# Sparse attention and a squared-ReLU expert on one core: half of the early casts moved into DMA transfers, and the masks of both halves made by VectorE products

## The chip, the cores and the metric

The kernel runs on one core of a Trainium2 chip. The metric is the device time of one execution in microseconds (us). Lower is better. Executions of one kernel lie within about 1.5% of each other. An execution more than 1.5% above the fastest of its kernel counts as slow and is not used. "Same" means a difference of less than 2%.

Words used below. PE is the matrix engine, DVE is VectorE, ACT is ScalarE, POOL is GpSimd, and SP is SyncE, which here only issues transfers. A *granted clock* of 1.00 means that PE ran at its full rate, and 0.5 that it got half of it. A *filler* is a matmul on zeros whose result nobody reads (`keep_warm`). It is there to keep PE busy. The *transposed q* of a batch (`qb<-scr_q`) comes, from batch 2 on, by a transposing transfer from a buffer in DRAM (`scr_q`), and the scores of that batch wait for it.

## The reference, cut to what matters

```python
# q, k, v: 8 batches x 8 heads x 576 tokens x 64, fp32; 8 global tokens; window 32
scores = q @ k.T / 8
mask = |i - j| <= 32  or  i is global  or  j is global
attn = softmax(where(mask, scores, -1e9))
x = (attn @ v) as 4608 tokens x 512          # heads side by side
h = x @ w_in                                 # 512 -> 2048
out = (relu(h) ** 2) @ w_out                 # 2048 -> 512, fp32
```

The expert's matmuls fill most of the time, and they can start only when the attention of the first half of batch 0 is done. The values of the global tokens are needed by every query, and the outputs of the global queries are written over their columns of x at the end (`scatter`).

## The kernel before: the parts that matter

Batch 0 (8 heads, handled as 4 pairs) is the start-up. Its k and q come as fp32 through transfers issued by SP, and DVE and ACT cast them. Then come transposes on PE, scores, exponentials, and outputs.

```python
for hp in range(NHP):                    # all 4 pairs of batch 0, fp32
    for nm in "kq":
        fetch_tokens(nc.sync, nm, 0, hp)
...                                      # cut: constants by affine_select on GpSimd
for x in range(NT):
    fetch_values(0, x)                   # GpSimd issues; the transfer casts to fp16
```

The mask of half 0 was added in PSUM by an identity matmul ahead of the scores. That of half 1 was multiplied in by DVE after the exponential.

```python
def mask_first(half, tag):
    sc = pst(tag, [P, 2, 512])
    for e in range(2):
        nc.tensor.matmul(sc[:, e, 0:W], identity, far[:, 0:W], start=True, stop=False, ...)
```

The values of the global tokens of batch 0 were gathered by one-hot matmuls, and copied by ACT and DVE (`v_globals`, one call for each pair). The global columns of x are written by `scatter`, whose columns are register values. They are loaded from SBUF by VectorE in `load_columns`, after two clamps each in `columns`.

```python
def load_columns(part):
    idx, top = {None: (g32c, S - 1), 0: (g32a, HS), 1: (g32b, S - 256)}[part]
    _, gvs[part] = nc.values_load_multi_w_load_instructions(
        idx[0:1, 0:NG], engines=[mybir.EngineType.DVE], ...)

def scatter(b, part=None, pairs=slice(0, NHP)):
    for g in range(NG):
        dve.tensor_copy(out=xT[:, pairs, lo:hi][:, :, ds(gvs[part][g], 1)],
                        in_=gxs[b][:, pairs, g : g + 1])
```

The order of the start-up, cut:

```python
mask_natural(0); gb = indices(); fetch_globals(); keep_warm(4); one_hots(gb); ...
cast_tokens(dve.tensor_copy, "k", 0); cast_tokens(act.copy, "q", 0)
mask_globals(mg, 0); transposes0(0); mask_added(0)
for nm in "kq":
    cast_tokens(dve.tensor_copy, nm, 1)          # pair 1
for i in range(4): pool.dma_start(out=w_in...)
for i in range(NHP):                             # transposes, scores, exp; keep_warm(1) each
    ...
for j in range(4): pool.dma_start(out=w_out...)
mask_natural(1); columns(); clear_ones(dve.memset, vb[0]); load_columns(0)
...                                              # outputs of half 0, with keep_warm(1) each
scatter(0, 0)
...                                              # batch 1's k, q, v are fetched from here on
scatter(0, 1)
take(99)                                         # expert matmuls of the queue
globals_in_place()                               # casts batch 1's and 2's global rows (DVE, ACT)
value_globals(1)                                 # SP: 5 small transfers into vb of batch 1
globals_to_scratch(2); tokens_to_scratch(2)
```

The softmax here doesn't subtract the row's maximum and nothing guards it: scores larger than these inputs give would overflow.

Of the kernel before, what the change touches and what calls it, by code (L numbers as in the profile page):

```python
# [42 lines left out]
SCHED = dict(h0=0, w=4, h1=2, h2=2, h3=0, p0=3, p1=1, p2=2, b1=((2, 1, 2), (1, 1, 2), (1, 1, 2), (1, 1, 2)))  # L43
# [4 lines left out]
def kernel(  # L48
# [41 lines left out]
    st = {nm: sbt("st" + nm, [TP, H, TJ, D], FP32) for nm in "kq"}  # L90
# [21 lines left out]
    def fetch_values(b, x, hs=slice(0, H)):  # L112
        back = NG if b == 0 and x else 0
        pool.dma_start(  # L114
            out=vb[b][NG - back : NG + KN[x], x, 2 * hs.start : 2 * hs.stop : 2],
            in_=v[b, hs, x * KT - back : x * KT + KN[x]].rearrange("h s d -> s h d"),
        )

    act.dma_start(out=g64, in_=global_idx.unsqueeze(0))
    for hp in range(NHP):  # L120
        for nm in "kq":
            fetch_tokens(nc.sync, nm, 0, hp)
    act.preload_act_table_set("natural_log_exp_and_others")

# [6 lines left out]
    pidx = sbt("pidx", [P, 4], I32)  # L131
    nc.gpsimd.iota(pidx, pattern=[[0, 4]], base=0, channel_multiplier=1)
    icb = sbt("icb", [P, 4], I32)
    nc.gpsimd.iota(icb, pattern=[[2 * H * S, 4]], base=2 * H * S, channel_multiplier=0)
    ig = sbt("ig", [P, NG], FP32)
    nc.gpsimd.iota(
        ig, pattern=[[1, NG]], base=0, channel_multiplier=0, allow_small_or_imprecise_dtypes=True,
    )

    U0 = 48  # L140
    UN = 208
    ub = [sbt(f"ub{i}", [P, UN], FP16) for i in range(2)]
    nc.gpsimd.memset(ub[0], 1.0)
    for base, cu, cm in (
        (-8, 0, 1), (window + U0 - 8, -1, 1), (window - U0 + 8, 1, -1),
    ):
        nc.gpsimd.affine_select(
            out=ub[0], in_=ub[0], compare_op=ALU.is_ge, fill=0.0,
            base=base, pattern=[[cu, UN]], channel_multiplier=cm,
        )  # L150
    rows = sbt("rows", [P, 2], FP16)
    nc.gpsimd.memset(rows, 1.0)
    for col, base, cm in ((slice(0, 2), -8, 1), (slice(1, 2), KN[-1] + 7, -1)):
        nc.gpsimd.affine_select(
            out=rows[:, col], in_=rows[:, col], compare_op=ALU.is_ge, fill=0.0,
            base=base, pattern=[[0, col.stop - col.start]], channel_multiplier=cm,
        )
    nc.gpsimd.affine_select(
        out=ub[1], in_=ub[0], compare_op=ALU.is_ge, fill=0.0,
        base=KN[-1] + 7, pattern=[[0, UN]], channel_multiplier=-1,  # L160
    )

    tok = sbt("tok", [P, NT], FP32)
    nc.gpsimd.iota(
        tok, pattern=[[KT, NT]], base=-8, channel_multiplier=1,
        allow_small_or_imprecise_dtypes=True,
    )
    nc.gpsimd.affine_select(
        out=tok, in_=tok, compare_op=ALU.is_ge, fill=-1.0,
        base=-8, pattern=[[0, NT]], channel_multiplier=1,  # L170
    )
    tokp = sbt("tokp", [P, TJ], FP32)
    nc.gpsimd.iota(
        tokp, pattern=[[1, TJ]], base=0, channel_multiplier=TJ,
        allow_small_or_imprecise_dtypes=True,
    )
    identity = sbt("identity", [P, P], FP16)
    nc.gpsimd.memset(identity, 0.0)
    nc.gpsimd.affine_select(
        out=identity, in_=identity, compare_op=ALU.not_equal, fill=1.0,  # L180
        base=0, pattern=[[-1, P]], channel_multiplier=1,
    )
    for kt in kts:
        dve.memset(kt[:, 4, 8 + KN[4] : P], 0.0)
# [4 lines left out]

    def clear_tail(op, t):  # L190
        op(t[96:P, NT - 1, 0 : 2 * H : 2], 0.0)

    clear_tail(dve.memset, vb[0])
    for x in range(NT):
        fetch_values(0, x)
# [78 lines left out]
    far = sbt("far", [P, SCW[0]], FP16)  # L274

# [12 lines left out]

    def mask_added(half):

        r = slice(MB[half], MB[half] + SCW[half])
        nc.vector.tensor_scalar(
            out=far[:, r], in0=mask[:, r], scalar1=-1.0, scalar2=100.0 / scale,
            op0=ALU.add, op1=ALU.mult,
        )



# [65 lines left out]
    grows = sbt("grows", [NG, 3, 2, H, D], FP32, bufs=2, tag="gt")  # L364
    grow = {nm: grows[:, i] for i, nm in enumerate("kqv")}
    g16s = {nm: sbt("g16s" + nm, [NG, 2, H, D], FP16) for nm in "kqv"}

    def fetch_globals():
# [3 lines left out]
        )  # L372
        for nm in "kqv":
            for g in range(NG):
                nc.sync.dma_start(
                    out=grow[nm][g : g + 1],
                    in_=src[nm][1:3, :, ds(at[g], 1), :].rearrange("b h o d -> o b h d"),
                )
# [74 lines left out]
    def v_globals(hp, op1=None, op2=None):  # L453
        vs = vb[0][:, :, 4 * hp : 4 * hp + 4 : 2]
        gl = pst("mm", [P, 512])[0:NG, 0 : 2 * D]
        for t in range(NT):
            nc.tensor.matmul(gl, oh[:, t, :], vs[:, t], start=(t == 0), stop=(t == NT - 1))
        gvs = sbt("gvs", [NG, 2 * D], FP16, bufs=2)
        (op1 or act.copy)(out=gvs, in_=gl)
        (op2 or dve.tensor_copy)(  # L460
            out=vs[0:NG],
            in_=gvs.rearrange("p (h d) -> p h d", d=D).unsqueeze(1).to_broadcast((NG, NT, 2, D)),
        )

    def transposed(nm, i, tag):
        b, hp = divmod(i, NHP)
        tr = pst(tag, [P, 1024], FP16)
        for j in range(TJ):
            n = TP + NG if (b and j == TJ - 1) else TP
            if b == 0:  # L470
                nc.tensor.transpose(
                    tr[:, TP * j : TP * j + n], nat0[(nm, hp)][:, j, :], identity[0:n, 0:n]
                )
            for e in range(2) if b else ():
# [5 lines left out]
        if b == 0:  # L480
            gl = tr.bitcast(FP32)[:, 384 : 384 + NG]
            for j in range(TJ):
                nc.tensor.matmul(
                    gl, nat0[(nm, hp)][:, j, :], ohp[0:TP, j, :],
                    start=(j == 0), stop=(j == TJ - 1), skip_group_check=True,
                )
# [134 lines left out]
    def mask_first(half, tag):  # L621
        sc = pst(tag, [P, 2, 512])
        W = SCW[half]
        for e in range(2):
            nc.tensor.matmul(
                sc[:, e, 0:W], identity, far[:, 0:W],
                start=True, stop=False, skip_group_check=True,
            )
        return sc

    def scores(i, half, tag, wins, sc=None):
        kt, qt = key_query(i)
        added = sc is not None
        if not added:
            sc = pst(tag, [P, 2, 512])
        for t, so, c0, w in wins[half]:
            for e in range(2):
# [3 lines left out]
                    start=not added, stop=True, skip_group_check=True,  # L641
# [3 lines left out]
    def weights(half, sc, wins, added=False):  # L645
# [5 lines left out]
        if not added:  # L651
            dve.tensor_tensor(  # L652
                out=et[:, :, 0:W], in0=et[:, :, 0:W],
                in1=mask[:, MB[half] : MB[half] + W].unsqueeze(1).to_broadcast((P, 2, W)),
                op=ALU.mult,
            )
# [275 lines left out]
```

## Time and profile before

| | before |
|---|---|
| time, median of 3 | 331.81 us (331.32 to 332.03) |
| span in the profile | 330.1 us |
| PE busy / DVE busy / ACT busy | 316.8 / 223.9 / 212.9 us |
| first expert matmul on tokens | 27.31 us |
| first scores of batch 2 | 69.66 us |
| mean granted clock | 0.999 |

The table of stretches of the kernel before has, for each stretch of time: its length, the busy time of each engine with the number of its instructions, the granted clock of PE, the mean busy share of the DMA engines, and GB/s.

```profile
0.00:8.25 8.25, 5.75 (x41) 2.37 (x42) 6.00 (x36) 4.06 (x11) 7.03 (x24) 1.00 0.79 210
8.25:16.50 8.25, 7.33 (x130) 5.11 (x130) 6.81 (x24) 6.24 (x18) 7.12 (x9) 1.00 1.79 196
16.50:24.75 8.25, 6.18 (x114) 4.40 (x114) 5.87 (x23) 5.67 (x19) 2.42 (x4) 1.00 1.27 205
...
41.00:50.00 9.00, 8.23 (x111) 5.54 (x112) 6.09 (x16) 5.87 (x13) 6.73 (x8) 1.00 2.23 161
...
70.00:330.00 260.00, 255.58 (x1616) 126.63 (x1610) 172.16 (x440) 166.98 (x320) 72.86 (x84) 1.00 0.90 99
```

The first number after the length is PE. In the last 260 us PE is 98% busy, so there is little to gain there. In the first 70 us it has gaps. The timeline of PE shows where it waits. A line gives start, length, engine, source line, operation, its tiles, and in brackets the idle time just before it and what ended that.

```profile
6.18 0.43 PE L471 MATMUL mm<-identity,nat0k 96*128 96x96 f16 x6
...
7.74 0.55 PE L625 MATMUL sc<-far,identity 128*128 128x456 f16 x2 [0.59 <-DVE far L292]
...
17.85 0.26 PE L672 MATMUL sc<-et,vb 128*64 128x160 f16 x2 [0.69 <-DVE vb L460]
...
27.31 1.92 PE L543 MATMUL mm<-xT,w_in 128*128 128x256 f16 x16
...
39.47 0.45 PE L475 MATMUL tr<-identity,natk 96*64 96x96 f16 x12 [0.51 <-DMA natk<-in_k_dram]
...
46.69 0.23 PE L672 MATMUL sc<-et,vb 128*64 128x88 f16 x2 [0.17 <-DMA vb<-in_v_dram]
...
49.10 0.25 PE L672 MATMUL acc<-et,vb 128*64 128x136 f16 x2 [0.52 <-DMA vb<-in_v_dram]
```

In the first 18 us of the start-up PE waits mostly for DVE, in pieces of at most 0.7 us. The last three lines are the waits for batch 1's data, 1.2 us in all, that the change aims at. The timeline of VectorE has the casts of pairs 0, 1 (k and q) and, later, the scatter of half 1 and the cast of the value rows of the global tokens:

```profile
5.36 0.77 DVE L449 CAST nat0k<-stk 96x768 f16<-96x768 f32 x1
...
7.61 0.54 DVE L449 CAST nat0k<-stk 96x768 f16<-96x768 f32 x1
8.51 0.56 DVE L449 CAST nat0q<-stq 96x768 f16<-96x768 f32 x1 [0.36 <-DMA stq<-in_q_dram]
...
34.30 1.65 DVE L751 COPY xT<-gx 128x4 f16 x8
...
37.95 0.68 DVE L383 CAST g16sv<-grows 8x1024 f16<-8x1024 f32 x1
```

The timeline of SyncE's queue has the five transfers that put these rows beside batch 1's values:

```profile
38.66 3.87 SPq L440 DMA_DIRECT2D vb<-g16sv  x5
```

### The profile page before, as it was taken

What the parts mean: (1) busy time and instruction counts of PE and PEld (TensorE: products, weight loads), DVE (VectorE), ACT (ScalarE), POOL (GpSimd) and SP (SyncE); (2) the same over time, 40 slices, a digit from 0 to 9 for tenths busy, and PEclk for the clock granted to TensorE, in tenths of its full rate; (3) what the DMA queues carried; (4) which work ended last, traced back from release to release, by engine and by line L of the source; (5) the groups of instructions that cost most, each with busy time, mean ns of one, the idle gap of its engine ahead of it and who ended that gap; (6) DMA issues with size and microseconds to landing.
All of it is one profiled execution on the core that took longest, in us unless ns stands there. A gap on an engine that the chain in (4) does not pass through costs nothing.

```text
span 330.1 us, 6785 instructions
## 1 busy us (share of the span) xinstructions
PE 316.8 (96%) x2393; PEld 165.4 (50%) x2393; DVE 223.9 (68%) x610; ACT 212.9 (64%) x425; POOL 107.6 (33%) x140
## 2 busy tenths in 40 slices
PE   6878999999999999999999999999999999999996
PEld 2656764445454545554545554545555444444444
DVE  7877965787768775877587758775887585323421
ACT  4767666669953995499549954995499536404700
POOL 8822477008900792077006920690000000000000
PEclk9999999999999999999999999999999999999999
DMA  7999999946998299999932999999610001011012
GB/s 210 196 205 208 202 160 140 150 143 68 138 148 192 19 138 161 170 105 128 158 124 52 125 139 159 140 127 158 111 66 1 32 34 64 0 66 64 1 47 82
DMA packets 148876, 38.20 MB, mean 116 GB/s; under 512 B 136818, under 2 KB 144362, under 8 KB 148842
## 3 DMA queue, kind: packets, MB, share of 16 engines
q0 software_dynamic: 104624, 17.37, 70.9%
q1 hardware_dynamic: 44072, 20.26, 31.1%
q8 instruction: 19, 0.31, 0.4%
q10 hardware_dynamic: 146, 0.13, 0.1%
q14 instruction: 15, 0.12, 0.1%
HBM read 37.36 MB, written 17.05 MB: 165 GB/s over the span
## 4 chain that ended last, share of the span: by engine, by line
PE 46%; ACT 23%; DVE 12%; DMA 9%; issue 6%; POOL 2%; SPq 0%; DVEq 0%; ACTq 0%; POOLq 0%
PE mm L587 22%; ACT rl L529 9%; PE mm L524 9%; ACT et L648 7%; PE tr L587 5%; DMA vb<-in_v_dram 5%; ACT rec L704 4%; DMA qb<-scr_q 4%; DVE xT L732 3%; PE tr L524 3%; ACT rec L705 2%; DVE et L652 2%; DVE xT L751 2%; PE sc L681 2%; DVE gt L530 2%
## 5 line engine op out<-in xcount | busy, mean ns | idle before, releaser
L587 PE MATMUL mm<-w_out,gt 128*128 128x512 f16 x448 | 104.9, 379 | 0.0
L524 PE MATMUL mm<-xT,w_in 128*128 128x512 f16 x384 | 90.8, 379 | 0.6 <-DVE xT L751 0.6
L587 PEld LDWEIGHTS <-gt 128*128 128x128 f16 x560 | 52.1, 98 | 58.1
L524 PEld LDWEIGHTS <-w_in 128*128 128x128 f16 x512 | 47.5, 98 | 53.9 <-issue 1.1
L529 ACT ACTIVATE rl<-mm 128x512 f16<-128x512 f32 x96 | 55.1, 600 | 26.4 <-PE mm L524 25.8
L530 DVE TENSOR_TENSOR gt<-rl 128x512 f16<-128x512 f16 x128 | 52.2, 423 | 16.6 <-ACT rl L529 14.4
L648 ACT ACTIVATE et<-sc 128x880 f16<-128x880 f32 (+1 forms) x32 | 29.0, 905 | 43.4 <-PE sc L639 43.4
L652 DVE TENSOR_TENSOR et<-et,mask 128x880 f16<-128x880 f16 x60 | 36.6, 615 | 26.8 <-ACT et L648 25.9
L114 POOL DMA_DIRECT2D vb<-in_v_dram x40 | 41.7, 1620 | 7.9 <-DMA w_out<-in_moe_w_out_dram 6.9
L524 PE MATMUL tr<-xT,w_in 128*128 128x512 f16 x128 | 32.9, 380 | 0.0
L564 DVE COPY ot<-mm 128x512 f32<-128x512 f32 (+1 forms) x29 | 19.7, 679 | 17.5 <-PE mm L587 15.8
L732 DVE TENSOR_TENSOR xT<-sc,rec 64x288 f16<-64x288 f32 (+1 forms) x56 | 25.5, 455 | 8.8 <-ACT rec L705 8.4
L890 POOL COPY pin<-gsh 1x1 f32<-1x1 f32 x5 | 0.9, 178 | 89.1 <-DVE gsh L720 89.1
L705 ACT ACTIVATE rec<-rec 128x288 f32<-128x288 f32 x64 | 28.3, 442 | 2.0
L648 ACT ACTIVATE et<-acc 128x880 f16<-128x880 f32 (+1 forms) x32 | 29.0, 908 | 0.2 <-PE acc L639 0.2
L732 DVE TENSOR_TENSOR xT<-acc,rec 64x288 f16<-64x288 f32 (+1 forms) x56 | 25.5, 455 | 5.1 <-ACT rec L705 4.7
L681 PEld LDWEIGHTS <-vb 128*128 128x128 f16 x288 | 21.4, 98 | 12.6 <-issue 2.0
L419 POOL DMA_DIRECT2D scr_k<-in_k_dram x30 | 26.6, 1098 | 2.6 <-DMA natq<-in_q_dram 1.7
L704 ACT ACTIVATE rec<-sc 64x288 f32<-64x288 f32 (+1 forms) x56 | 22.8, 407 | 6.5 <-PE sc L681 4.2
L587 PE MATMUL tr<-w_out,gt 128*128 128x512 f16 x112 | 25.3, 379 | 0.0
L419 POOL DMA_DIRECT2D scr_q<-in_q_dram x24 | 24.9, 1591 | 0.7 <-DMA vb<-in_v_dram 0.6
L704 ACT ACTIVATE rec<-acc 64x288 f32<-64x288 f32 (+1 forms) x56 | 22.6, 404 | 1.9 <-PE acc L672 1.1
(135 smaller groups left out, 297.2 us busy)
## 6 DMA issues: line engine op xcount, KB each, us to landing
out_dram<-ot SPq DMA_DIRECT2D x35, 256.0 KB
vb<-in_v_dram POOLq DMA_DIRECT2D x29, 120.0 KB, 10.9
scr_q<-in_q_dram POOLq DMA_DIRECT2D x24, 144.0 KB, 5.5
scr_k<-in_k_dram POOLq DMA_DIRECT2D x24, 120.0 KB, 4.2
w_in<-in_moe_w_in_dram POOLq DMA_DIRECT2D x4, 512.0 KB, 14.1
w_out<-in_moe_w_out_dram POOLq DMA_DIRECT2D x4, 512.0 KB, 17.5
stk<-in_k_dram SPq DMA_DIRECT2D x4, 288.0 KB
stq<-in_q_dram SPq DMA_DIRECT2D x4, 288.0 KB
```

The costliest lines, as they stand in the source:

```text
L114: pool.dma_start(out=vb[b][NG - back : NG + KN[x], x, 2 * hs.start : 2 * hs.stop : 2], in_=v[b, hs, x * KT - back : x * KT + KN[x]].rearra ...
L419: pool.dma_start(out=scr[(nm, b % 2)][x * pitch + off : x * pitch + off + hi - lo].rearrange("s (h d) -> s h d", d=D), in_=src[nm][b, :, l ...
L524: nc.tensor.matmul(ph, w_in[:, t, u * P : (u + 1) * P], xT[:, t, XOFF + c * TC : XOFF + (c + 1) * TC], start=(t == 0), stop=(t == NDM - 1),)
L529: nc.scalar.activation(out=rl, in_=ph, func=AF.Relu)
L530: nc.vector.tensor_tensor(out=gts[c][:, u, :], in0=rl, in1=rl, op=ALU.mult)
L587: nc.tensor.matmul(po, gts[c][:, f, m * P : (m + 1) * P], w_out[:, f, :], start=(f == 0), stop=(f == NFF - 1),)
L648: act.activation(out=et[:, :, 0:W], in_=sc[:, :, 0:W], func=AF.Exp, bias=0.0, scale=scale)
L652: dve.tensor_tensor(out=et[:, :, 0:W], in0=et[:, :, 0:W], in1=mask[:, MB[half] : MB[half] + W].unsqueeze(1).to_broadcast((P, 2, W)), op=AL ...
L681: nc.tensor.matmul(acc[:, e, o : o + w], vtf[:, t, vo : vo + P], et[:, e, so : so + w], start=(n == 0), stop=(n == nw - 1), skip_group_che ...
L704: act.activation(out=rec[r], in_=av[rs, xs, :, 0:GTOK], func=AF.Ln)
L705: act.activation(out=rec, in_=rec, func=AF.Exp, scale=-1.0)
L732: dve.tensor_tensor(out=xT[r, hp, x0 : x0 + HS].rearrange("p (k x) -> p k x", k=2), in0=av[r, x, :, 0:GTOK], in1=rec[r], op=ALU.mult,)
```

## The change

The intent is to take work off the engines of the start-up. Half of batch 0's k and q (pairs 2 and 3) comes by transfers that cast, so that four DVE casts go. The mask of half 0 becomes a VectorE product like that of half 1, so that eight identity matmuls go. The value rows of batch 0's global tokens are fetched directly, and cast once on ACT, so that 20 matmuls and four chains of copies go. Batch 1's k, q and v are transferred ahead of w_out. The constants are made by DVE from iotas, and GpSimd starts its transfers earlier. The fillers and the order of units were set anew. The diff, cut to its core:

```diff
-    for hp in range(NHP):
+    for hp in range(2):
         for nm in "kq":
             fetch_tokens(nc.sync, nm, 0, hp)
...
-    (constants by affine_select on GpSimd)
+    (iotas on GpSimd)
+    for nm in "kq":
+        fetch_tokens(pool, nm, 0, 2, 2)
+    for x in range(NT):
+        fetch_values(0, x)
+    def constants():                    # DVE: identity, ub, rows, tok
...
-    def mask_first(half, tag): ...
-        (weights(): no product when the mask was added)
+        dve.tensor_tensor(out=et..., in0=et..., in1=mask..., op=ALU.mult)   # always
...
-    def v_globals(hp, op1=None, op2=None): (one-hot matmuls, ACT and DVE copies)
+    def v_globals():
+        act.copy(out=gv16, in_=gv0)
+        for x in range(NT):
+            dve.tensor_copy(out=vb[0][0:NG, x, 0 : 2 * H : 2], in_=gv16)
...
+    constants()
     one_hots(gb)
     cast_tokens(dve.tensor_copy, "k", 0)
     cast_tokens(act.copy, "q", 0)
+    mask_natural(0)
+    transposes0(0)
+    mg = mask_globals_matmul(0)
+    mask_globals(mg, 0)
+    columns()
+    load_columns(0)
+    cast_tokens(dve.tensor_copy, "k", 1)
+    cast_tokens(dve.tensor_copy, "q", 1)
+    keep_warm(SCHED["w3"])
+    tr_k(1, ...); keep_warm(SCHED["w4"]); tr_q(1, ...)
...
+    (w_in, then batch 1's k, q and v, then w_out)
+    v_globals()
+    half0(2); half0(3)
+    half0_out(0, "mm"); half0_out(1, "sc"); half0_out(2, "acc"); half0_out(3, "mm")
...
-            dve.tensor_reduce(out=gsum[b][:, half, hp], ...)
+            for x in range(2):
+                dve.tensor_reduce(out=gsum[b][:, half, hp, x], ...)
```

## The prediction

> **What bounds it now.** The page gives PE 96% busy of a 330.1 us span at full granted clock, but the shortfall sits at the front. In the timeline of PE the first expert matmul on real tokens starts at 27.3 us; before it PE does batch 0's attention (half of it) and warm-up matmuls. From 70 us on PE is busy 97 to 99% (stretch table), and nothing in the change removes matmuls there, so I take that part as constant. DMA is the second limit: in the records of single transfers the 16 engines are busy from 3.2 us until about 58 us without a gap: batch 0 k and q (1536-byte packets, 178 to 200 per us, to 11.6), v (128-byte, 1120 per us, landed 16.66), w_in and w_out (190 per us, to 37), batch 1 k/q (260 per us, to 43), batch 1 v (to 47, last piece waited for until 49.1), then batch 2. Batch 2's transposed q lands near 68.3; PE uses it at 69.66, so only about 1.3 us of slack.
>
> **What changes.** (1) Half of batch 0's k and q arrives by casting transfers: 768 packets at 260 per us instead of 178 to 200, about 1.2 us less engine time. The Trainium skill ("DMA: Bandwidth & Descriptors", SWDGE vs HWDGE vs iDMA) says each engine round-robins between queues; this trace differs: v, issued from 4.7 us, moved its first packet only at 11.5, when the direct queue was empty. By that order v should land at about 14.7 instead of 16.66. (2) Batch 1 k/q/v go ahead of w_out: at 31 and 35 us instead of 43 and 47. That removes PE's waits for DMA at 39.5, 46.7 and 49.1 (0.51+0.17+0.52 = 1.2 us). (3) Removed: mask matmuls (8, about 0.27 each) and the 20 value-global matmuls with four chains of ACT 0.26 and DVE 0.4; four DVE casts of 0.56. (4) Added: four DVE mask products of 0.64, VectorE constants (about 1.7 us before the one-hots), a doubled tensor_reduce (60 more of 0.19), index arithmetic and clears moved to the batch-1 units.
>
> **Critical path.** I chained the new order with durations of the trace. Constants delay the first k cast by about 0.6 us; pair 1 casts wait behind masks; exps of pairs 2 and 3 wait on ACT behind q copies and the value-global cast. First half-0 output: about 18.8 us (before 17.85), although v is early: ACT and DVE bind, not v. Then four Ln/Exp pairs, scatter (1.65 us) and products as before: expert matmuls start near 27.4, about where they did. So the start gains nothing, the DMA waits give 1.2 us back, and more DVE work in 50 to 70 us (about 3 us, PE already waits for DVE 1.1 us there) takes about 0.5. The doubled reduces fall into DVE's wait for the Exp (0.28 us). Net about -0.7, a little more allowed for tuned fillers: **330.6 us, 327.8 to 333.2**. Faster by over 2%: 5%; within: 91%; slower: 4%.
>
> **What would show it.** v landing 14 to 15.5; first expert matmul 26 to 29; no PE wait for a DMA between 35 and 50; DVE busy about 235 us (223.9 now); the span after 70 us unchanged within 0.7 us.
>
> **What would make it wrong.** Global value rows landing late (32 small SP transfers at 0.75 us each instead of 24), stalling ACT at the value-global cast, or DVE's cast of batch-1 globals near 36 us; a start 2 to 3 us earlier because DVE/ACT overlap better than chained; batch 2's transposed q landing after PE wants it.

One correction to its text. The times of single transfers in it (3.2, 11.6, 37, 43, 47, 58 and 68.3 us) were read with a zero that lay 1.35 us too early, so they are about 1.35 us too high on the scale of the other views. Differences between two of them are not touched. But the slack of 1.3 us for batch 2's transposed q sets 68.3 against 69.66 from the timeline of PE, so on one scale it is about 2.7 us. And the direct queue was not quite empty when the first packet of v moved: 70 of its 1536 packets were still to come.

## The result, and the profile after

| | before | after |
|---|---|---|
| time, median of 4 | 331.56 us (330.60 to 332.03) | 334.77 us (334.06 to 335.48) |
| ratio | | 1.010 (1.0067 to 1.0134) |
| span in the profile | 330.1 us | 333.7 us |
| PE / DVE / ACT busy | 316.8 / 223.9 / 212.9 us | 319.6 / 230.7 / 211.4 us |
| first half-0 outputs | 17.85 us | 19.35 us |
| first expert matmul on tokens | 27.31 us | 28.68 us |
| first scores of batch 2 | 69.66 us | 73.43 us |
| mean granted clock, each run | 0.999 (profiled run) | 0.974 in all four |

A ratio is the mean time of one kernel's fast runs over that of the other's of the same rounds, with its 95% interval, so it is not quite the ratio of the two medians. The changed kernel is 1.0% slower. That is "same" by the 2% rule, but it is outside the predicted range, whose upper end was 333.2 us.

The table of stretches of the kernel after:

```profile
0.00:8.25 8.25, 5.93 (x41) 2.47 (x41) 5.85 (x35) 3.48 (x10) 7.48 (x22) 1.00 0.86 194
8.25:16.50 8.25, 6.49 (x129) 4.91 (x131) 5.36 (x17) 3.73 (x12) 4.83 (x7) 0.66 1.81 179
16.50:24.75 8.25, 7.28 (x134) 6.18 (x133) 6.91 (x27) 6.79 (x14) 4.09 (x5) 0.52 1.27 204
...
41.00:50.00 9.00, 7.24 (x98) 5.42 (x99) 6.87 (x20) 6.21 (x13) 5.03 (x6) 0.91 1.93 174
...
70.00:330.00 260.00, 258.56 (x1632) 128.04 (x1630) 177.40 (x500) 168.09 (x324) 72.72 (x84) 1.00 0.90 97
```

Read the clock column first: 0.66 and 0.52 where it was 1.00. The last line is not a slower steady state. The kernel after reaches 70 us with more work left (1632 instead of 1616 matmuls remain), and does it at the same rate. The timeline of PE after, with the answers to the lines shown above:

```profile
6.67 0.60 PE L195 MATMUL tr<-idle 128*128 128x512 f16 x2
9.25 0.43 PE L453 MATMUL mm<-identity,nat0k 96*128 96x96 f16 x6 [1.97 <-DVE nat0k L435]
...
13.92 0.69 PE L457 MATMUL mm<-identity,natk 96*64 96x96 f16 x12
...
19.35 0.34 PE L648 MATMUL mm<-et,vb 128*64 128x160 f16 x2 [0.67 <-DVE vb L444]
...
39.05 1.92 PE L528 MATMUL mm<-xT,w_in 128*128 128x256 f16 x16 [0.66 <-DVE xT L729]
...
46.63 0.26 PE L648 MATMUL sc<-et,vb 128*64 128x160 f16 x2 [0.44 <-DVE gt L540]
...
48.02 0.27 PE L648 MATMUL sc<-et,vb 128*64 128x192 f16 x2 [1.05 <-DMA vb<-g16sv]
...
48.64 0.28 PE L648 MATMUL sc<-et,vb 128*64 128x88 f16 x2 [0.27 <-DMA vb<-g16sv]
```

Three things are to be seen. There is one wait of 1.97 us at 9.25 us, for the cast of pair 1's k. The transposes at 13.92 us took 0.69 us for twelve, against 0.45 for the same form in the kernel before. The waits for batch 1's tokens and values are gone, as intended, but there are new ones in the same place: for the *global rows* of the values (`vb<-g16sv`), for DVE and for the scatter, 2.4 us in all.

The clock record gives the times of the half clock. It changes only at the edges of windows of 3.413 us. In the kernel before it was full from 4.9 us to the last matmuls. In the kernel after it was half from 10.81 to 24.47 us, which is four windows, and again from 48.36 to 51.77 us, which is one. This is the record for the windows of the kernel after, beside PE's busy share worked out from its instructions:

| window of after, us | PE busy share | clock in it | clock in the next |
|---|---|---|---|
| 3.99 to 7.40 | 0.92 | full | full |
| 7.40 to 10.81 | 0.45 | full | **half** |
| 10.81 to 14.23 | 0.78 | half | half |
| 14.23 to 17.64 | 1.00 | half | half |
| 17.64 to 21.05 | 0.72 | half | half |
| 21.05 to 24.47 | 1.00 | half | full |
| 44.95 to 48.36 | 0.56 | full | **half** |
| 48.36 to 51.77 | 0.92 | half | full |

Both drops came right after a window in which PE waited: for most of the 1.97 us, and for 1.49 us in two pieces (0.44 and 1.05; the wait of 0.27 came after the edge at 48.36). In the kernel before the lowest share of any window up to 73 us was 0.69.

The timeline of VectorE after shows what made PE wait at 7.3 us:

```profile
4.54 0.80 DVE L435 CAST nat0k<-stk 96x768 f16<-96x768 f32 x1
...
5.36 0.54 DVE L250 COPY mask<-rows 128x8 f16<-128x8 f16 x1
...
5.95 0.81 DVE L250 COPY mask<-rows 128x8 f16<-128x8 f16 x3
...
7.00 0.65 DVE L215 TENSOR_SCALAR g32b<-g 1x8 int32<-1x8 int32 x1
7.69 0.16 DVE L216 TENSOR_SCALAR g32b<-g32b 1x8 int32<-1x8 int32 x1
8.63 0.56 DVE L435 CAST nat0k<-stk 96x768 f16<-96x768 f32 x1 [0.79 <-DVE g32b L216]
...
36.54 2.45 DVE L729 COPY xT<-gx 128x4 f16 x8
...
40.50 0.68 DVE L369 CAST g16sv<-grows 8x1024 f16<-8x1024 f32 x1
```

Ahead of the cast at 8.63 stand four clamps (`columns`) and then 0.79 us in which DVE executes nothing that counts as busy. That is the load of eight registers (`load_columns(0)`). The timeline leaves it out, and puts the idle time down to the clamp before it, the load's input. The view of the load's source line has it, for the kernel after and then for the kernel before (count, shortest, median and longest in ns, start in us):

```profile
L719 DVEq TENSOR_LOAD <-g32a x1: 847/847/847, 7.7 to 7.7; - x1
```

```profile
L741 DVEq TENSOR_LOAD <-g32a x1: 839/839/839, 15.6 to 15.6; - x1
```

The load is as long in the kernel before, but there DVE had five memsets issued ahead of it (1.36 us from 15.78), which ran meanwhile, so that it left no idle time on DVE. The timeline also shows slow copies: a copy of eight columns took 0.54 us, a clamp of eight numbers 0.65 us. The same forms take 0.16 and 0.15 elsewhere. They are slow while GpSimd issues transfers, as its timeline in the kernel after shows:

```profile
3.99 4.45 POOL L113 DMA_DIRECT2D vb<-in_v_dram  x5
```

And the timeline of SyncE's queue after, with the five transfers of the global rows 2.5 us later than before:

```profile
41.20 3.83 SPq L426 DMA_DIRECT2D vb<-g16sv  x5
```

### The profile page after: what moved, and what is told of

The parts are those of the page before. It is cut to its first block, busy times and chain, and to the rows that moved or that the text cites. A ratio compares the mean times of both kernels' runs of the same rounds, so it can differ in the third digit from the quotient of the medians.

```text
span 333.7 us, 6906 instructions
## 1 busy us (share of the span) xinstructions
PE 319.6 (96%) x2418; PEld 168.4 (50%) x2418; DVE 230.7 (69%) x681; ACT 211.4 (63%) x417; POOL 106.2 (32%) x137
## 4 chain that ended last, share of the span: by engine, by line
PE 77%; DMA 7%; DVE 7%; SPq 3%; ACT 3%; issue 2%; DVEq 0%
PE mm L509 25%; PE mm L572 24%; PE tr L509 9%; PE tr L572 5%; DMA qb<-scr_q 4%; PE sc L657 3%; PE acc L657 3%; PE sc L612 2%; DVE xT L729 2%; SPq L356 2%; DMA vb<-g16sv 2%; PE mm L528 2%; PE acc L612 1%; DMA grows<-in_k_dram 1%; DVE xT L710 1%
## 5 line engine op out<-in xcount | busy, mean ns | idle before, releaser
L624 DVE TENSOR_TENSOR et<-et,mask 128x880 f16<-128x880 f16 (+1 forms) x64 | 38.9, 614 | 24.6 <-ACT et L621 23.4
```

The costliest lines, as they stand in the source:

```text
L624: dve.tensor_tensor(out=et[:, :, 0:W], in0=et[:, :, 0:W], in1=mask[:, MB[half] : MB[half] + W].unsqueeze(1).to_broadcast((P, 2, W)), op=AL ...
```

## The experiments

Sixteen runs were made (two of them repeats), in four groups, each group on one chip beside the kernel before. All gave correct outputs. The theories were these. **Clock**: the gap at 7.3 us halves the clock, and that costs the time. **Order**: VectorE's order (clamps and register load ahead of pair 1's casts) makes the gap. **Port**: DVE's copies are slow while GpSimd issues transfers, and so the start is late. **Late values**: the global rows of batch 1 come late, and make the second loss at 46 to 50 us. **Vector work**: the doubled reduces and the mask products load DVE too much.

The results in one table. "Half clock" is from the clock record of the profiled execution. mm1 is the first expert matmul on tokens, b2 the first score of batch 2. All of these kernels but before_order and before_cold have done one expert step of 0.87 us more than before at b2.

| run | ratio to before (95%) | medians, this / before | mm1 | b2 | half clock, us |
|---|---|---|---|---|---|
| after | 1.0100 (1.0067 to 1.0134) | 334.77 / 331.56 | 28.68 | 73.43 | 10.81–24.47, 48.36–51.77 |
| fill_idle | 1.0061 (1.0036 to 1.0086) | 334.95 / 332.66 | 26.23 | 70.91 | none |
| late_load | 0.9984 (0.9944 to 1.0023) | 331.90 / 332.66 | 24.88 | 69.69 | 17.61–21.02, 44.92–48.33 |
| early_values | 1.0028 (1.0004 to 1.0052) | 333.54 / 332.66 | 29.29 | 71.94 | 9.21–26.28 |
| both_moves | 1.0009 (0.9979 to 1.0039) | 332.54 / 332.66 | 25.16 | 69.89 | 16.59–20.01, 37.07–40.49 |
| late_issue | 1.0046 (1.0005 to 1.0087) | 333.52 / 331.47 | 27.80 | 70.59 | 10.71–24.36 |
| before_order | 1.0051 (1.0004 to 1.0099) | 333.66 / 331.47 | 28.69 | 70.74 | from the start to 13.52 |
| work_in_wait | 1.0007 (0.9965 to 1.0049) | 331.68 / 331.47 | 25.70 | 68.80 | 15.47–22.30 |
| one_reduce | 1.0090 (1.0047 to 1.0134) | 334.43 / 331.47 | 29.54 | 72.23 | 9.51–26.57 |
| after_again | 1.0091 (1.0057 to 1.0125) | 335.04 / 331.71 | 29.70 | 72.53 | 9.63–26.70 |
| fill_again | 1.0065 (1.0021 to 1.0109) | 333.57 / 331.71 | 26.59 | 71.56 | 17.72–21.13, 38.20–41.61 |
| before_cold | 1.0020 (0.9984 to 1.0057) | 333.18 / 331.71 | 31.15 | 72.41 | 7.79–11.21, 18.03–31.69 |
| combined | 0.9985 (0.9945 to 1.0024) | 331.53 / 331.71 | 26.33 | 69.34 | none |
| late_fill | 1.0028 (0.9978 to 1.0078) | 334.07 / 332.32 | 28.05 | 73.00 | 11.49–21.73 |
| late_gate | 0.9949 (0.9906 to 0.9993) | 331.33 / 332.32 | 25.68 | 68.53 | 16.55–19.97, 105.3–108.7 |
| late_fill_gate | 1.0011 (0.9957 to 1.0066) | 331.76 / 332.32 | 24.97 | 69.49 | none |
| late_all | 1.0048 (1.0002 to 1.0093) | 333.64 / 332.32 | 27.63 | 73.18 | 16.45–19.87, 47.17–50.59 |

A word on the noise. At each change of batch PE may wait for the transposed q (`qb<-scr_q`). This wait hits any kernel and varies: 0.47 us at 204.65 in the profile of before, 0.71 at 140.95 in that of after, 2.41 at 104.4 in that of late_gate, none in that of after_again. The kernel before also ran in some executions with a mean clock of 1.000 and in others with 0.985 to 0.990: in the last group its three executions at 0.985 took 333.6 to 334.2 us, and six of the eight at 1.000 took 330.9 to 332.3. This mean does not count the time before the clock's first record, so an execution that starts cold for longer does not show in it: before_order's profile has a mean of 0.998, but its first record only at 13.52 us, and its transposes took 0.64 to 0.69 us until then and 0.42 after. So a difference of less than about 0.3% in one group is not to be read.

### fill_idle: keep PE busy through the gap

```diff
-SCHED = dict(... w3=2 ...)
+SCHED = dict(... w3=11 ...)      # nine more fillers ahead of pair 1's transposes
```

> The changed kernel with 11 instead of 2 warm-up matmuls ahead of pair 1's key transposes, so that TensorE is busy in the idle of 7.3 to 9.25 us; no wait is taken away. Theory CLOCK (the gap lets the granted clock fall to half for about 13.6 us, and that delays the first expert matmul): the clock stays 1.00 in the first 25 us (it was 0.66 and 0.52 in the second and third stretch of 8.25 us), the first expert matmul comes at 27.3 to 28 us instead of 28.68, and the time falls by 0.7 to 1.4 us from 334.8. Theory LATE VALUES (the loss is the wait for batch 1's value globals at 46 to 49 us): the time moves by less than 0.5 us. Theory VECTOR WORK (more VectorE instructions): no change.

The clock stayed full for the whole run, and the expert started 2.45 us earlier (26.23 instead of 28.68). The time gained much less: 1.0061 against 1.0100. The earlier start ran into the scatter of half 1. Here are that scatter's line in the timeline of VectorE of fill_idle, and the wait in its timeline of PE:

```profile
34.09 3.71 DVE L729 COPY xT<-gx 128x4 f16 x8
```

```profile
37.86 1.92 PE L528 MATMUL mm<-xT,w_in 128*128 128x256 f16 x16 [1.93 <-DVE xT L729]
```

The eight small copies took 3.71 us instead of 1.65, because they now fell into the time when GpSimd issues batch 2's transfers. PE then waited another 1.6 us for transfers ahead of batch 1's first outputs at 45 to 47 us, and 2.7 us in all for the transposed q of two later batches. At b2 this profile was 2.5 us ahead of that of the kernel after, and 2.0 us of that went into longer waits for the transposed q (2.74 us against 0.71). As these waits vary from one execution to the next, the ratio is the better measure: the clock is part of the loss, but by the ratio not most of it. The intervals of fill_idle and of after overlap, so even that part is not shown clear of noise by the times.

### late_load: clamps and register load after pair 1's casts

```diff
     mask_globals(mg, 0)
-    columns()
-    load_columns(0)
     cast_tokens(dve.tensor_copy, "k", 1)
...
     half0(1)
+    columns()
     mg = mask_globals_matmul(1)
...
+    load_columns(0)
     v_globals()
```

> The changed kernel with VectorE's clamps and the register load of the scatter columns moved from ahead of pair 1's casts to behind the first mask products. Theory CLOCK: VectorE casts pair 1 about 1 to 1.9 us earlier (unless its transfer is only just there), TensorE's idle of 1.97 us shrinks under 1 us, the clock stays 1.00 up to 25 us, the first expert matmul at 26.5 to 27.7, time lower by 1 to 2 us. Theory LATE VALUES: as much of that as reaches the wait at 46 to 49 us is lost again there, time lower by at most 0.5 us. Theory VECTOR WORK: no change, as the same instructions run.

This one move takes the whole loss away: 0.9984 instead of 1.010. The timeline of VectorE of late_load shows pair 1's k cast 1.87 us earlier than in the kernel after (8.63): 0.79 us for the load and 1.08 for the clamps, of which one was slow. The run moved both and does not part them further. Its timeline of PE shows the gap gone:

```profile
6.76 0.56 DVE L435 CAST nat0k<-stk 96x768 f16<-96x768 f32 x1
7.87 0.56 DVE L435 CAST nat0q<-stq 96x768 f16<-96x768 f32 x1 [0.55 <-DMA stq<-in_q_dram]
```

```profile
7.08 0.60 PE L195 MATMUL tr<-idle 128*128 128x512 f16 x2
7.52 0.42 PE L453 MATMUL mm<-identity,nat0k 96*128 96x96 f16 x6
```

The first expert matmul came at 24.88 us, 2.4 us before that of the kernel before. Yet the time only equals that of the kernel before. The clock fell for one window at 17.61, and for one at 44.92, each after a window with a busy share below 0.6 (0.55 and 0.59). PE still waited 0.63, 0.36 and 0.42 us for the global rows, and for DVE in batch 1. Which of these takes how much of the 2.4 us is not settled.

### early_values: batch 1's global rows cast and sent before the scatter

```diff
     half1_out(3)
+    dve.tensor_copy(out=g16s["v"], in_=grow["v"])
+    value_globals(1)
     scatter(0, 1)
     take(99)
     globals_in_place()             # without the cast of "v"
-    value_globals(1)
```

> The changed kernel with the cast of batch 1's value globals and their five SyncE transfers moved ahead of the scatter of the second half (VectorE at about 36 instead of 40.5 us). Theory LATE VALUES: TensorE's waits for these transfers (1.05 and 0.27 us at 48 us) go, the second drop of the clock (0.93 and 0.89 in 41 to 60 us) goes with them, and the time falls by 2 to 3 us to about 332. Theory CLOCK (first drop only): under 0.5 us. Theory VECTOR WORK: no change.

The first transfer of the rows was issued at 37.91 instead of 41.20 us, and every wait for them was gone, with the second drop of the clock. The gap at the start and its half clock stayed (9.21 to 26.28). The ratio is 1.0028, about 0.7% better than after. Its interval and that of after do not overlap. So the late rows are a second cause, apart from the first. The gain has a price: the cast now ahead of the scatter made PE wait 1.15 us for the scatter instead of 0.66.

### both_moves: late_load and early_values together

The edits are those two.

> Both moves together. If the first clock drop and the late value globals are the whole loss, the gains add: 330 us or less, 1.00 of the clock throughout, at or under the kernel before (331.6). If VECTOR WORK costs something of its own, it stays over 331.6 although the clock is full.

The gains do not add: 1.0009, no better than late_load alone. With the earlier start, PE waited 1.67 us for the scatter of half 1 at 36.54, which took 2.60 us under GpSimd's issues, and the clock fell for the window after it.

### late_issue: GpSimd's transfers of batch 0's values issued later

```diff
-    for x in range(NT):
-        fetch_values(0, x)
...
     cast_tokens(dve.tensor_copy, "q", 1)
+    gate = sbt("gate", [P, 1], FP32)
+    pool.tensor_copy(out=gate[0:1], in_=nat0[("q", 1)][0:1, TJ - 1, P - 1 : P])
+    for x in range(NT):
+        fetch_values(0, x)
```

> The changed kernel with GpSimd's five value transfers of batch 0 (and all that follow them on its queue) held back until VectorE has cast pair 1. In the changed kernel's trace every VectorE copy, cast or one-input operation that is more than 0.12 us over its usual time (14 of them, 4.7 us in sum; 6 and 1.5 us in the kernel before) overlaps a GpSimd DMA issue, and between 4.5 and 7.7 us they hold up pair 1's casts. Theory PORT (the overlap is the cause): between 4.5 us and the casts none of them is slow, pair 1's first cast ends about 1 to 2 us earlier than 9.2 us, TensorE's idle of 1.97 us falls under 1.2, the clock stays 1.00 to at least 16 us, and the time falls by 0.5 to 2 us unless the values then land later than TensorE asks for them (17 to 19 us). Rival (the slow copies come from the transfers' own writes, or from the register load): the same copies stay slow, the gap stays near 2 us.

This tests the port theory alone: the order on DVE is that of the kernel after, only GpSimd is silent between 4.5 and 8.3 us. In the timeline of VectorE of late_issue the same three operations took 0.55, 0.31 and 0.56 us, where the kernel after had 0.80, 0.81 and 0.56:

```profile
4.53 0.55 DVE L432 CAST nat0k<-stk 96x768 f16<-96x768 f32 x1
...
5.59 0.31 DVE L247 COPY mask<-rows 128x8 f16<-128x8 f16 x3
...
7.77 0.56 DVE L432 CAST nat0k<-stk 96x768 f16<-96x768 f32 x1 [0.78 <-DVE g32b L213]
```

All DVE operations up to 8.3 us had their usual lengths, and pair 1's cast began at 7.77 instead of 8.63. So the slow copies are real and are made by GpSimd's issues, and they cost 0.86 us there. That the writing of the values slows them can be ruled out: in the kernel after the first packet of the values moved at 8.91 us, when these copies were done. The register load's 0.78 us remained. The gap shrank from 1.97 to 1.04 us, but the clock still fell, after a window with a busy share of 0.46. Both causes of the gap are needed to explain its size. The ratio of 1.0046 is not apart from that of one_reduce in the same group (1.0090), as the intervals overlap.

### before_order: the kernel before with only the order of transfers changed

```diff
-    for j in range(4):
-        pool.dma_start(out=w_out[:, ts(j, 4), :], ...)
     mask_natural(1)
...
     for x in range(NT):
         fetch_values(1, x)
+    for j in range(4):
+        pool.dma_start(out=w_out[:, ts(j, 4), :], ...)
```

> The kernel before with nothing changed but the order of transfers: w_out behind batch 1's keys, queries and values. The prediction gave this alone 1.2 us, the sum of TensorE's three waits for DMA at 39.5, 46.7 and 49.1 us. If that was right, the waits go and the time falls by about 1.2 us (ratio 0.996). Theory LATE VALUES: the wait for batch 1's value globals, which SyncE issues at 38.7 to 42.5 us in this kernel, takes their place in part, and the time falls by 0.5 us or less. A rise of the time would say that w_out now comes too late or that GpSimd's issues collide with VectorE's scatter.

The prediction counted 1.2 us of gain for this part, and none is to be seen: 1.0051. How much the order itself costs is not settled by it, since the profiled execution began with the half clock up to 13.52 us, which has nothing to do with this edit and makes its start 1.4 us later. Whether the other five executions did so too is not recorded. The profile gives one hint that is free of the cold start: from mm1 to b2, with the same work, it took 42.05 us, and the kernel before 42.35. So 0.3 of the 1.2 us was gained there, in one execution. It also shows where the rest would have gone. Of the three DMA waits 0.46 us was left, at 48.65, and PE waited 0.80 us at 38.51 for the scatter of half 1, three of whose copies ran into GpSimd's next issues and took 0.43, 0.67 and 0.55 us instead of 0.18. That wait is one that the prediction missed, and here it is without the rest of the change.

### work_in_wait: late_load, with more expert steps ahead of batch 1's first outputs

```diff
 (late_load's moves)
-b1=((2, 1, 2), (2, 1, 2), (1, 1, 2), (2, 0, 4))
+b1=((4, 1, 2), (2, 1, 2), (1, 1, 2), (1, 0, 3))
```

> late_load with four instead of two half-chunk units of the first expert layer ahead of batch 1's first outputs (one or two fewer later), so that TensorE has real work in its waits for the value globals (0.63, 0.36 and 0.42 us at 43 to 45 us in late_load) and the clock has no cause to drop at 45 to 48 us. Theory LATE VALUES with CLOCK: those waits fall under 0.4 us in sum, the clock is 1.00 from 41 us on, the time 1.5 to 3 us under late_load's (ratio to before about 0.990 to 0.994). If the ratio stays at 0.998, the waits only moved.

The waits for the global rows and the second drop of the clock were gone, and b2 came at 68.80. The time did not follow (1.0007): PE waited for DVE instead, 0.95 us at 36.36, 0.52 at 58.6, 1.08 at 65.07 and 0.85 at 70.2. DVE is what batch 1's units lean on, so filling one wait moves it to the next.

### one_reduce: the kernel after with one reduce instead of two for batches 1 to 7

```diff
-            for x in range(2):
-                dve.tensor_reduce(out=gsum[b][:, half, hp, x], in_=av[x]..., ...)
+            dve.tensor_reduce(out=gsum[b][:, half, hp], in_=whole..., ...)
```

> The changed kernel with the split tensor_reduce put back to one instruction for batches 1 to 7 (56 fewer instructions on VectorE, each pair 0.26 us against 0.19 for one). Theory VECTOR WORK: the time falls by 0.5 us or more. The prediction held these to lie in VectorE's wait for the Exp: time as the changed kernel's within 0.3% (ratio to before 1.008 to 1.012).

The ratio is 1.0090, that of after. The groups of instructions by form show a single reduce of 191 ns in the kernel before and two of 170 ns in the kernel after (count, then busy us and mean ns). First before, then after:

```profile
L720 DVE TENSOR_REDUCE gsh<-sc 128x16 f32<-128x32 f32 x28 | 5.4, 191 | 11.8 <-ACT rec L704 9.9 <-PE acc L681 1.9
```

```profile
L698 DVE TENSOR_REDUCE gsh<-sc 128x8 f32<-128x16 f32 x56 | 7.2, 170 | 12.7 <-ACT rec L680 12.3 <-PE acc L657 0.5
```

After them DVE waits for ACT's Exp in any case. From 70 to 330 us the products that follow the reduces (`xT<-sc,rec`, `xT<-acc,rec`) waited for it 10.0 us in one_reduce and 5.2 us in the kernel after (waits over 0.15 us), so the added reduces lie in that wait. The theory of vector work in the steady state falls. The four mask products of the start were not tested alone.

### after_again and fill_again: the same two kernels on another chip

No edit: the kernel after and fill_idle once more, in one group.

> The changed kernel unaltered, as the control of these runs on one chip. Ratio to before 1.008 to 1.012, mean granted clock 0.972 to 0.979, first expert matmul 28 to 29.5 us.

> fill_idle once more, beside its control. Theory CLOCK: 0.3 to 0.7% under after_again, in a profile at full clock the first score of batch 2 about 2.5 us earlier. If it shows no difference to after_again, the half clock of the first 25 us costs nothing in the whole time.

The ratios repeat: 1.0091 and 1.0065, after 1.0100 and 1.0061. So the loss of the change is about 0.95%, on two chips. The fillers alone seem to bring about 0.3% of it back on both, but the intervals overlap each time. In after_again the half clock was there from 9.63 to 26.70, five windows, and the second drop was not. In fill_again two single windows were at half clock, which fill_idle did not have. That would fit drops that depend on where the fixed windows fall on the program: PE's waits near 48 us left a busy share of 0.56 in the window from 44.95 in after, and of 0.64 in that from 47.18 in after_again, which no drop followed. It is not shown beyond that.

### before_cold: the kernel before without twelve of its fillers

```diff
     fetch_globals()
-    keep_warm(4)
...
-        keep_warm(1)        # after each pair's scores (4)
...
-        keep_warm(1)        # after each pair's outputs (4)
```

> The kernel before without its 12 warm-up matmuls after the first six (the four after the index broadcast and one after each pair in two loops). Theory CLOCK turned round: TensorE's busy share of a window of 3.4 us in the first 10 us falls under about 0.6, the clock goes to half for at least two windows within the first 25 us, mean clock 0.97 to 0.985, the first expert matmul comes 1 to 2.5 us after 27.3, and the time rises by 1 to 2.5 us (ratio 1.003 to 1.008), although no work and no wait was added. If the clock stays full or the time stays, the fillers and the clock matter less than I say.

This puts the cold clock into the kernel before, without any of the change. In the profiled execution the clock was half from 7.79 to 11.21 and from 18.03 to 31.69, and the expert began at 31.15, 3.8 us later. At the last matmul 2.2 us of that were left. Only this execution had a mean clock of 0.974. The other five had 0.990 to 1.000, and their median was lower by about 0.9 us. The ratio of 1.0020 is therefore no measure of a cold start. The profile suggests that part of a late start is made up for later, where PE would otherwise have waited: the lag behind the kernel before was 3.8 us at mm1 and 2.7 at b2. But it is one execution against one.

### combined: everything that had helped, together

late_load, late_issue, more fillers (`w3=5`, `w4=2`, three ahead of pair 0's scores, four ahead of the first outputs), `b1=((3, 1, 2), (2, 1, 2), (2, 1, 2), (1, 0, 3))`, the index arithmetic earlier, and GpSimd's issues of batch 2 held back until the scatter is done. The last part is:

```diff
     globals_to_scratch(2)
+    pool.tensor_copy(out=gate[0:1], in_=xT[0:1, 0, XOFF + 300 : XOFF + 301])
     tokens_to_scratch(2)
```

> All that the runs pointed to, on the changed kernel: value transfers held back until pair 1 is cast (late_issue), register load later (late_load), index arithmetic in VectorE's early idle instead of the batch-1 units, a few more warm-up matmuls in TensorE's waits, one more unit of expert work ahead of batch 1's first outputs, and batch 2's casting transfers held back until the scatter is done. If PORT, CLOCK and LATE VALUES are the whole loss: clock 1.00 up to 40 us, first expert matmul at 24 to 25.5 us, first score of batch 2 under 69 us, ratio to before 0.990 to 0.997. If it stays at 1.00 or over, something that I have not named takes the gain back.

The clock was full throughout, and yet the ratio is 0.9985: the same as late_load alone, and short of what I expected. The waits turned up elsewhere: 1.43 us for DVE's mask product at 25.8, 0.45 and 0.32 for the global rows, and 0.63 at 20.9, 0.49 at 64.7 and 0.60 at 69.3 for DVE. The later issue did not remove the slow copies but moved them (11 of them, 3.05 us beyond their usual times).

### late_fill, late_gate, late_fill_gate, late_all: late_load with single additions

This group took the largest help, late_load, and added one thing at a time: five fillers before the first outputs and six before batch 1's first (late_fill), the gate on GpSimd shown above (late_gate), both (late_fill_gate), and both with the index arithmetic moved early (late_all).

```diff
+    keep_warm(5)                       # late_fill
     half0_out(0, "mm")
...
+        if i == NHP: keep_warm(6)      # late_fill, in unit()
...
+    pool.tensor_copy(out=gate[0:1], in_=xT[0:1, 0, XOFF + 300 : XOFF + 301])   # late_gate
     tokens_to_scratch(2)
...
+    index_base()                       # late_all, after half0(1)
     columns()
```

> late_load with 5 warm-up matmuls ahead of the first outputs of batch 0 and 6 ahead of the first outputs of batch 1, the two places where its clock fell. If the half clock takes late_load's earlier start back: clock 0.997 or more, first score of batch 2 at 68 to 69 us (69.7 in late_load), ratio to before 0.992 to 0.996. If not: ratio 0.997 to 1.001 at full clock.

> late_load with GpSimd's transfers for batch 2 held back until the scatter of the second half is done. If the collision matters: the scatter takes 1.65 us instead of 2.1 and up, TensorE's wait for it near 35 us goes, ratio 0.2 to 0.4% under late_load's 0.998. If not, no change; if batch 2's transposed queries now land late, TensorE waits for them near 70 us and it is slower.

> Both of the last. If the two losses are apart they add: ratio 0.990 to 0.994. If it stays near 0.998, a third thing holds the time.

> late_fill_gate with the index arithmetic in VectorE's idle near 14 us instead of in the batch-1 units. If VectorE's added work in those units holds the time: TensorE's waits for VectorE at 58 to 71 us fall under 0.5 us in sum and the ratio is 0.2 to 0.4% under late_fill_gate's. If not, equal to it.

late_fill was a fault of my own design. The filler writes a PSUM bank that a DVE copy still reads, so the filler itself waited 1.78 us, and the ratio went to 1.0028. late_fill_gate and late_all have the same fault, with ratios of 1.0011 (full clock in the profiled run) and 1.0048. The fault is not all of it. In the profiled run of late_fill the clock fell at 11.49 us, ahead of any added filler. And of its six executions the two at a mean clock of 1.000 took 331.64 and 331.93 us, fault and all, the four at 0.982 to 0.995 took 333.44 to 335.41. So about 3 us went with the state of the clock in one and the same kernel, though fill_idle's executions show no such order. late_all shows how sensitive the front is: seven small DVE operations in front of the copies of kt made PE wait 1.43 us at 15.7. Its fillers waited 1.78 us as well, so the 1.0048 is not the work of the seven alone.

late_gate is the best of all: 0.9949, with an interval that just excludes 1. The timelines of GpSimd and of VectorE of late_gate show the gate at work, with the copy that waits for the scatter, and the scatter ahead of it in 1.90 us (2.08 in late_load):

```profile
35.51 0.30 POOL L833 CAST gate<-xT 1x1 f32<-1x1 f16 x1 [0.89 <-DVE xT L729]
35.76 4.53 POOL L405 DMA_DIRECT2D scr_k<-in_k_dram  x5
```

```profile
33.55 1.90 DVE L729 COPY xT<-gx 128x4 f16 x8
```

It took out the 0.30 us for which PE had waited for the scatter in late_load, and b2 came at 68.53, the earliest of all. The intervals of late_load and late_gate overlap, so that the gate helps beyond late_load is not shown, and the best of sixteen runs may owe something to chance. By the 2% rule no version here beats the kernel before.

## Why the prediction was wrong, point by point

**The steps that failed.** The prediction said that "expert matmuls start near 27.4, about where they did. So the start gains nothing", and then "the DMA waits give 1.2 us back".

1. *The start.* The chain was added up from full-clock durations and usual DVE durations, in an order where "pair 1 casts wait behind masks". Measured: the expert began at 28.68 (29.70 in after_again). The constants did not delay the first cast (4.54, against 5.36 before). What came instead was one gap of 1.97 us on PE at 7.3 us, since pair 1's cast waited behind four clamps and an exposed register load of 0.79 us, with copies made slow by GpSimd's issues. I had costed neither. late_load, which takes only clamps and load away from there, removes the loss: from 1.0100 and 1.0091 to 0.9984. late_issue shows that the slow copies add 0.86 us.

   That the start came out near the forecast, 28.68 where 26 to 29 was named, and the first outputs at 19.35 where 18.8 was, is in part luck. With the clock kept full the new order gave 17.39 and 26.23 (fill_idle), and 24.88 for the expert without the gap (late_load). The chain was too long by about 1.2 us or more, and the half clock, which it did not have, covered that.

   The gap then closed the clock gate. The Trainium skill ("TensorE: Matmul & The Clock Gate", Part 1) gives a free-running window of 3413 ns and a drop to half rate after one idle window. This trace agrees on the window: all changes lie 3.413 us or a multiple of it apart. It differs on the rest. A gap of 1.97 us was enough, in a window that was 45% busy, and after it four windows passed before the clock was full, though they were 72 to 100% busy. The prediction took the clock of the kernel before for granted and never asked whether the new order had a long gap. The fillers alone (fill_idle, fill_again) give back about 0.3% of the 0.95%, within the noise.

2. *The DMA waits.* The order of transfers did what was predicted. PE no longer waits for batch 1's tokens or values, and the records of single transfers show that batch 0's value rows are all but moved by 13.2 us instead of 15 and batch 1's k and q by 31 instead of 43. The sum that was wrong is the gain. New waits took the place of the old: 1.05 + 0.27 us for the global rows of the values, 0.44 for DVE and 0.66 for the scatter, 2.4 us in all where 1.2 had been. The rows came late since DVE cast them at 40.50 instead of 37.95. I had named this risk ("landing late ... DVE's cast of batch-1 globals near 36 us"), but put it outside of the sum. early_values shows its size: about 0.7%. In before_order the new order alone gained nothing in the time, though a cold start blurs that run.

3. *What was not in the sum at all: the port.* The Trainium skill ("SBUF — State Buffer", Who interferes with whom) says that VectorE's `copy`, `cast` and `tensor_scalar` can take a port pair that GpSimd needs too, and that the one that comes first holds it while the other is blocked. I looked at GpSimd's transfers for their place in the queue only. The trace agrees: every copy, cast or tensor_scalar that ran over 0.12 us beyond its usual time overlaps an issue of a transfer by GpSimd: 6 operations with 1.5 us beyond their usual times in the kernel before, 14 with 4.7 us in the kernel after. The reverse does not hold: 33 others in the kernel after that lay in an issue for over half of their time were not slow. Products of two inputs were not slowed (423 ns with and without). Moving these issues changed the times (late_issue), so it is shown that the issues slow the copies. That the port pair is the way they do it is the skill's account; no run here tests it.

**What was right.** v was no longer what the first outputs wait for: they waited for DVE (`vb L444`), as predicted, though the time of it owes something to luck (see 1). The doubled reduces cost nothing (one_reduce). The last part is about as fast as before: from b2 to the end it took 260.2 us, and 260.4 in the kernel before, which had one step of 0.87 us more to do there. DVE's busy time was 230.7 us, where about 235 was predicted. As said, no PE wait for batch 1's k, q or v was left.

**What stays open.** The 3.2 us between the medians cannot be split exactly among clock, order, port and late rows. By the two profiles, 3.6 us apart, 1.4 us was lost up to mm1, and 1.5 more up to b2, without the step of 0.87 us that the kernel after does earlier; the last 0.7 came after b2. The single repairs are worth about 0.3% (fillers), 0.5% (late_issue), 0.7% (early_values) and 1.1% (late_load), the first two within the noise, and they do not add, since each moves the next wait. Why late_load, which starts the expert 2.4 us before the kernel before, ends at the same time, is also open in its parts. Half clock for two windows, waits for the global rows (1.41 us) and waits for DVE in batch 1 were seen in its profile. And I have no rule for when the clock drops. In the 18 profiles, up to 320 us, 23 windows at full clock had a busy share under 0.60, and 18 of them were followed by the half clock. The other five, with shares of 0.48 to 0.59, were not (fill_idle at 36.47 and 104.74, late_issue at 44.84, late_fill at 45.62, late_gate at 23.38), and two drops followed shares of 0.60 (fill_again, 14.30) and 0.75 (work_in_wait, 12.06).

## What to carry to other kernels

A chain of durations read from a kernel without long gaps holds only while the new order has none either. When a change reorders the start, first list PE's waits in the new order, look for a window of some 3.4 us in which PE would be less than about 60% busy (18 of 23 such windows here were followed by the half clock, and 18 of the 20 drops came after one), and treat fillers and order as part of the change. On VectorE, put register loads and other work that nobody waits for behind the casts that PE waits for, and keep GpSimd's issues of transfers away from the small copies on the critical path. A wait that is taken away pays only if the next thing that ends the wait is early too, so cost the next releaser before counting the gain.

## What the Trainium skill lacked or had wrong

- "TensorE: Matmul & The Clock Gate" (Part 1; Why this matters for your kernels) advises against gaps of more than about 3 us and has the clock drop after an idle window. Here a gap of 1.97 us, or two waits of 1.49 us in all, in a window that was 45% or 56% busy, was enough. A much lower limit for the gap would serve better. The busy share of the window is a guide, but not a sharp one (18 of 23 windows under 0.60).
- The same page has the full clock back after one busy window of about 3.4 us. Here it took four windows (13.65 us) in the kernel after and five in after_again, with busy shares of 0.72 to 1.00 in the kernel after. A single window sufficed for the later drops (48.36 to 51.77).
- "SBUF — State Buffer" (the box in "SBUF: two separate sides") warns that VectorE's copies starve GpSimd's descriptors. The other direction, which its rule allows, was what cost time here: copies of 0.16 us took up to 0.66, and scatters of eight copies 2.45 and 3.71 us instead of 1.65, while GpSimd issued transfers. For VectorE's side the page has only a "6.8× slower" in passing; the copies here took up to 4.2 times their usual time.
- "DMA: Bandwidth & Descriptors" (Latency and other measured facts) has a floor of about 600 ns for a `tensor_load`. This trace agrees: its TENSOR_LOAD records on VectorE, each of eight registers from SBUF, took 0.60, 0.61 and 0.85 us in the kernel after. The longest left that engine idle for 0.79 us. No page on VectorE says that such a load holds up what comes behind it.
- "DMA: Bandwidth & Descriptors" (SWDGE vs HWDGE vs iDMA; Queues, rings and completion order) has each engine serve its queues in turn. In the kernel before, values issued by GpSimd from 4.67 us moved their first packets at 10.2 us, when those of the direct queue were running out, and so it was in the kernel after (GpSimd's k and q from 2.46 us, first packets at 5.5). In late_issue, where the direct queue was done, the values' first packet moved 1.6 us after the issue. How the two kinds of queue share an engine was not tested further.
